# GpSimd takes the two-operand steps of the token routing, VectorE a share of the normalising, in a fused attention and mixture-of-experts kernel

## The chip, the cores and the metric
One core of a Trainium2 chip. Its engines run side by side, each with its own queue in program order: TensorE (PE, with its weight loads as PEld), VectorE (DVE), ScalarE (ACT), GpSimd (POOL), and SyncE (SP), which issues most transfers. The metric is the device time of one execution in microseconds; lower is better. TensorE's granted clock was at its upper level (1.00 of 2.4 GHz) in every 20 us of the profiled execution but the last, with a mean of 0.993.

## The reference
Causal attention for 4 batches of 12 heads, 448 tokens, head size 64. Its output, 1792 tokens of 768 values, goes through a layer of 8 experts of which each token uses one:
```python
scores = np.where(mask, -1000000000.0, scale * np.matmul(q, k.transpose(0, 1, 3, 2)))
attn = np.exp(scores - max); attn = attn / (sum(attn) + 1e-09)
x = np.matmul(attn, v)                            # per head, then 1792 x 768
logits = x @ w_gate + modality_bias[modality_id]
e_idx = np.argmax(logits, axis=1)
gate_w = softmax(logits)[np.arange(N), e_idx]
for e in range(E):
    mask = e_idx == e
    h = np.maximum(x[mask] @ w1[e], 0.0)
    out[mask] = gate_w[mask, None] * (h @ w2[e])
```

## The kernel before
The order of work is written out by hand. The attention loop has one turn n for each of the 48 heads, and each turn holds steps of several heads at once: `st_scores` of head n, `st_exp` of head n-1, `st_trans` and `st_split` of n-2, `st_pv` of n-3, `st_out` of n-4. All products are made of two parts (high and low) of each operand, so that GpSimd has to split q and k (`split_qk`, `split_kl`, one pair of heads every two turns) and v (`split_vh`, `split_vl`, every four turns). SyncE then stacks the parts of q and k by transfers within SBUF (`stack_qk`), for the scores two to four turns later, and a new q/k load starts when `split_kl` has freed one of two raw tiles.

Four heads make a group, three groups a batch. In turn n the token tile i of an older group gr (gr, i = divmod(n-8, 4)) is normalised: `st_comb` (TensorE) has put four heads' values and their share of the logits of a token tile (64 tokens in tile 0, 128 in tiles 1 to 3) in PSUM; for tiles 0 and 2 VectorE reads PSUM and multiplies by the reciprocal sums (`norm_l` for the logits, L407, `norm_x` for the values, L417); for tiles 1 and 3 ScalarE first copies them to SBUF (`st_move`, L399) and GpSimd multiplies there.

When a batch's last tile is normalised (turns 19, 31 and 43 for batches 0 to 2, after the loop for batch 3), `after_batch` spreads the steps of `route` over the turns that follow: the logits are summed, the largest found (`top`), subtracted (`centre`), the first expert among equals taken (`ties`, `first_tie`, `choice`), and TensorE counts places by matmuls with the choice (`places`). Then `slots`, `ranks` and `gates` give each token its slot in a table and its gate weight, and `scatter` writes four tables by indirect transfers on GpSimd's queue. `later(n, f)` puts a step behind the scores of turn n, `before(n, f)` ahead of them, `soon(n, f)` ahead of `st_split` of turn n; steps put at the same place run in the order in which they were put there. After batch 1 the expert with most tokens is known (`first_expert` and the following steps in turns 37 to 43), its weights are loaded, and in turns 45 to 47 GpSimd splits the first of them (`w1_chunk`, L672 and L673). Everything after about 240 us is the experts' matmuls.

Of the kernel before, what the change touches and what calls it, by code (L numbers as in the profile page):

```python
# [21 lines left out]
def attention_moe(  # L22
# [74 lines left out]
    sls = [cst(f"sl{j}", [128, NTL, E + 1]) for j in range(2)]  # L97
# [297 lines left out]
    def st_move(gr, i):  # L395
        if i % 2:
# [39 lines left out]
    def route(b):  # L436
        lg = sm([128, NTL, E], "lg")
        m = sm([128, NTL], "m")
        eq = sm([128, NTL, E], "eq")
        m2 = sm([128, NTL], "m2")  # L440
        oh = sm([128, NTL, E], "oh", BF16)
        pe = sm([128, NTL, E], "pe")
# [11 lines left out]
        def centre():  # L454
            V.tensor_tensor(out=lg, in0=lg, in1=wide(m), op=ALU.subtract)

        def ties():
            V.scalar_tensor_tensor(out=eq, in0=lg, scalar=0.0, in1=e8, op0=ALU.is_ge, op1=ALU.mult)
# [4 lines left out]
        def choice():  # L463
            V.tensor_tensor(out=oh, in0=eq, in1=wide(m2), op=ALU.is_equal)
            V.memset(oh[64:128, 0, :], 0.0)

        def places():
# [13 lines left out]
            A.activation(out=pe, in_=lg, func=AF.Exp)  # L481
            rt[b] = (pc, si)

        def slots():
            V.tensor_tensor(
# [4 lines left out]
        def ranks():  # L490
            V.tensor_reduce(out=sr, in_=sl, axis=AX, op=ALU.add)
            V.tensor_scalar(out=zs, in0=zs, scalar1=1e-9, scalar2=None, op0=ALU.add)

        def gates():
            V.tensor_copy(si, sr)
            V.reciprocal(out=ent[:, b, :, 1].bitcast(F32), in_=zs)
# [8 lines left out]
        sr = sm([128, NTL], "sr")  # L505
        return (logits, top, centre, ties, first_tie, choice), places, (slots, ranks, gates), scatter
# [29 lines left out]
    def first_base():  # L536
        V.tensor_scalar(out=eboff, in0=ebneg, scalar1=now[:, 2:3], scalar2=None, op0=ALU.add)
        V.tensor_scalar(out=eb64, in0=ebneg, scalar1=now[:, 3:4], scalar2=None, op0=ALU.add)
# [18 lines left out]
    def first_tri():  # L557
        V.tensor_scalar(out=n0, in0=oh0, scalar1=-1.0, scalar2=1.0, op0=ALU.mult, op1=ALU.add)
        V.tensor_tensor(out=tri0, in0=ctri, in1=eb(n0, E), op=ALU.mult)

    def first_order():
        V.tensor_tensor(out=tri0, in0=tri0, in1=eb(oh0, E), op=ALU.add)
        V.tensor_tensor(out=tri0, in0=tri0, in1=n0.rearrange("p (e o) -> p e o", o=1).to_broadcast([128, E, E]), op=ALU.mult)
# [310 lines left out]
    with tc.manual_schedule():  # L874
# [49 lines left out]
        V.memset(onesf, 1.0)  # L924
        V.memset(sch_a, -float(NT))
# [3 lines left out]
        for j in range(2):  # L929
            V.memset(sls[j], 0.0)  # L930
# [477 lines left out]
```

## Time and profile before
| | us |
|---|---|
| three timed executions | 504.43, 504.71, 505.88 |
| median | 504.71 |
| the profiled execution | 501.38 |
| its span, from the first to the last instruction | 499.7 |

Engines' busy time in the span: PE 476.8 us (95%), DVE 301.4 (60%), ACT 279.6 (56%), POOL 239.7 (48%). These are means over two parts: up to about 200 us, attention, in which PE, DVE, ACT and POOL are all busy for most of the time, and the experts after it, in which PE alone is. In rows of the profile a name such as L407 is a line of the kernel, `out<-in` are tiles by their names, and `[1.38 <-DVE oh L465]` says that the engine had been idle for 1.38 us until that instruction released it.

### The profile page before, as it was taken

To read this page: it belongs to the slowest core of one execution; us is meant where nothing else is said; L and a number is where in the kernel's file an instruction comes from. 1 tells how busy PE (TensorE), PEld (TensorE's weight loads), DVE (VectorE), ACT (ScalarE), POOL (GpSimd) and SP (SyncE) were. 2 spreads that over 40 slices of the span, in tenths; PEclk is the share of its full clock that TensorE was granted. 3 is DMA by queue.
4 is the path that set the end of the run, shared out by engine and by line. 5 is a ranking of instruction groups with operands and counts; after the bars stand their busy time and mean duration, and the time that the engine had idled before them with its cause. 6 is when DMAs were issued, how large, how long until landed. Compare 5 with 4: busy or idle time off the path is not lost.

```text
span 499.7 us, 10352 instructions
## 1 busy us (share of the span) xinstructions
PE 476.8 (95%) x3359; PEld 441.5 (88%) x3359; DVE 301.4 (60%) x893; ACT 279.6 (56%) x690; POOL 239.7 (48%) x292
## 2 busy tenths in 40 slices
PE   8999999999999988999999999999999999999990
PEld 5798999989988967878999999999999999888770
DVE  7899999999999999888412027441121120283580
ACT  5799999999988977616311216522121211383670
POOL 5899999999999889760311103202001001021131
PEclk9999999999999999999999999999999999999997
DMA  6887789987987889572396303863001001076100
GB/s 179 237 220 199 194 221 271 276 208 203 287 213 197 175 196 307 183 130 51 109 380 241 98 1 112 285 238 98 32 1 55 33 1 64 31 282 228 62 15 6
DMA packets 43817, 78.92 MB, mean 158 GB/s; under 512 B 15582, under 2 KB 27614, under 8 KB 43744
## 3 DMA queue, kind: packets, MB, share of 16 engines
q1 hardware_dynamic: 40704, 67.06, 47.5%
q0 software_dynamic: 3040, 11.03, 6.4%
q8 instruction: 28, 0.46, 0.4%
q14 instruction: 45, 0.37, 0.3%
HBM read 48.10 MB, written 11.89 MB: 120 GB/s over the span
## 4 chain that ended last, share of the span: by engine, by line
PE 71%; DVE 14%; DMA 6%; issue 3%; ACT 2%; POOL 1%; DVEq 0%; POOLq 0%; SPq 0%; ACTq 0%
PE g L748 7%; PE g L749 7%; PE g L750 7%; PE pt L297 6%; PE sb L266 4%; PE sa L266 4%; PE ot L336 3%; PE ot L329 3%; PE x L389 3%; DVE pl L316 3%; DVE p L275 2%; PE ot L750 2%; PE ot L749 2%; PE x L750 2%; PE x L749 2%
## 5 line engine op out<-in xcount | busy, mean ns | idle before, releaser
L285 ACT ACTIVATE p<-p,nm 128x448 f32<-128x448 f32 x192 | 94.8, 498 | 3.4 <-DVE nm L275 3.4
L729 POOL DMA_INDIRECT xg<-xs,idg x18 | 20.9, 1161 | 157.6 <-DVEq L1318 79.3
L767 DVE SCALAR_TENSOR_TENSOR htl<-g,hth 128x256 fp32r<-128x256 f32 x40 | 16.7, 424 | 103.8 <-ACT hth L766 103.8
L748 PE MATMUL g<-xh,w1h 128*128 128x256 f32 x240 | 67.1, 280 | 0.5 <-DVE htl L767 0.5
L749 PE MATMUL g<-xl,w1h 128*128 128x256 f32 x240 | 67.0, 279 | 0.0
L750 PE MATMUL g<-xh,w1l 128*128 128x256 f32 x240 | 67.0, 279 | 0.0
L297 PE MATMUL pt<-ident,p 128*128 128x128 f32 x432 | 63.2, 273 | 0.0
L316 DVE TENSOR_TENSOR pl<-pt,ph 128x1024 fp32r<-128x1024 f32 x48 | 58.3, 1215 | 7.0 <-ACT ph L315 6.8
L329 PE MATMUL ot<-ph,vhl 128*128 128x448 f32 x192 | 50.1, 301 | 3.9 <-DVE ut L360 3.7
L315 ACT ACTIVATE ph<-pt 128x1024 fp32r<-128x1024 f32 x48 | 49.0, 1020 | 7.8 <-PE pt L297 7.3
L297 PEld LDWEIGHTS pt<-ident,p 128*128 128x128 f32 x432 | 52.1, 147 | 1.2 <-issue 0.2
L766 ACT ACTIVATE hth<-g 128x256 fp32r<-128x256 f32 x40 | 15.1, 384 | 62.8 <-PE g L750 62.8
L748 PEld LDWEIGHTS g<-xh,w1h 128*128 128x128 f32 x240 | 45.1, 188 | 0.7 <-DVE htl L767 0.7
L749 PEld LDWEIGHTS g<-xl,w1h 128*128 128x128 f32 x240 | 45.1, 188 | 0.0
L750 PEld LDWEIGHTS g<-xh,w1l 128*128 128x128 f32 x240 | 45.1, 188 | 0.0
L808 POOL DMA_INDIRECT out_dram<-row,idg x14 | 16.4, 1173 | 59.6 <-ACTq L1302 33.5
L329 PEld LDWEIGHTS ot<-ph,vhl 128*128 128x128 f32 x192 | 32.8, 190 | 7.0 <-DVE ut L360 5.7
L275 DVE CUSTOM_DVE_ANT_0 p<-sa,mask 128x448 f32<-128x448 f32 x96 | 36.2, 413 | 2.3 <-PE sa L266 1.8
L285 ACT ACTIVATION_READ_ACCUMULATOR p<-p,nm 128x1 f32 x192 | 36.5, 190 | 0.0
L275 DVE CUSTOM_DVE_ANT_0 p<-sb,mask 128x192 f32<-128x192 f32 x96 | 36.3, 411 | 0.0
L336 PE MATMUL ot<-pl,vhl 128*64 128x64 f32 x192 | 34.4, 294 | 0.0
L354 ACT ACTIVATE hol<-ot 64x448 f32<-64x448 f32 x48 | 26.0, 542 | 11.2 <-PE ot L329 9.6
(348 smaller groups left out, 1340.1 us busy)
## 6 DMA issues: line engine op xcount, KB each, us to landing
st<-hl SPq DMA_DIRECT2D x56, 224.0 KB
raw<-in_moe_w_dram SPq DMA_DIRECT2D x24, 512.0 KB
raw<-in_qk_dram SPq DMA_DIRECT2D x21, 448.0 KB
raw<-in_moe_w_dram SPq DMA_DIRECT2D x20, 384.0 KB
vraw<-in_v_dram SPq DMA_DIRECT2D x12, 384.0 KB
xs<-row SPq DMA_DIRECT2D x12, 384.0 KB
w1h<-hl SPq DMA_DIRECT2D x14, 224.0 KB
w1l<-hl SPq DMA_DIRECT2D x14, 224.0 KB
```

The lines of the kernel that those rows point to most:

```text
L266: nc.tensor.matmul(outs[i], lhsT=a[:, q0:q0 + n], rhs=z[:, :w], start=(last == 0), stop=(last == 1 or qh is None))
L275: V.tensor_tensor_reduce(out=z, in0=o, in1=m, scale=-scale, scalar=3.0e38, op0=ALU.add, op1=ALU.min, accum_out=nm[:n, i:i + 1],)
L285: A.activation(out=z, in_=z, func=AF.Exp, bias=nm[:n, i:i + 1], scale=-1.0, accum_out=sums[:n, b, i, h:h + 1],)
L297: nc.tensor.transpose(out=o, in_=a, identity=ident)
L315: A.activation(out=ph, in_=t, func=AF.Copy)
L316: V.tensor_tensor(out=pl, in0=t, in1=ph.bitcast(F32), op=ALU.subtract)
L329: nc.tensor.matmul(o[:, q0:S], lhsT=t[:rows, kt, h].rearrange("p a d -> p (a d)"), rhs=ph[:rows, c0:c1], start=(n == 0), stop=(n == 1),)
L336: nc.tensor.matmul(o[0:D, q0:S], lhsT=t[:rows, kt, h, 0], rhs=pl[:rows, c0:c1], start=False, stop=False)
L354: A.activation(out=t, in_=ov[g][64:128, :S], func=AF.Copy)
L748: nc.tensor.matmul(o, lhsT=ah, rhs=bh, start=first, stop=False)
L749: nc.tensor.matmul(o, lhsT=ah, rhs=bl, start=False, stop=False)
L750: nc.tensor.matmul(o, lhsT=al, rhs=bh, start=False, stop=last)
```

## The change
In the loop's batches 0 to 2 GpSimd does the steps `ties` (with the subtraction that was `centre`), `choice` and the product of `slots`; batch 3 has the same code on VectorE. Two constants with a ninth column take the place of steps: `eq` holds 0.5 there, so that unused tokens get no choice without a memset, and `pe` holds 1e-9, so that the sum needs no addition. `ranks` reduces by the maximum straight into integers, so `gates` goes. `first_base`, `first_tri` and `first_order` move to GpSimd. Token tile 1 is normalised by VectorE from PSUM, except in the last two groups. The steps of the choice are placed at turns n+1 (two), n+2, ahead of n+3, and n+3.
```diff
     def st_move(gr, i):
-        if i % 2:
+        if i == 3 or i == 1 and gr >= B * NG - 2:
...
     def route(b):
         lg = sm([128, NTL, E], "lg")
+        G = V if b == B - 1 else P
...
-        def centre():
-            V.tensor_tensor(out=lg, in0=lg, in1=wide(m), op=ALU.subtract)
-
         def ties():
-            V.scalar_tensor_tensor(out=eq, in0=lg, scalar=0.0, in1=e8, op0=ALU.is_ge, op1=ALU.mult)
+            G.tensor_tensor(out=lg, in0=lg, in1=wide(m), op=ALU.subtract)
+            G.tensor_scalar(out=eq[:, :, 0:E], in0=lg, scalar1=0.0, scalar2=0.0, op0=ALU.is_equal, op1=ALU.add)
+            G.tensor_tensor(out=eq[:, :, 0:E], in0=eq[:, :, 0:E], in1=e8v, op=ALU.mult)
...
         def choice():
-            V.tensor_tensor(out=oh, in0=eq, in1=wide(m2), op=ALU.is_equal)
-            V.memset(oh[64:128, 0, :], 0.0)
+            ev = eq[:, :, 0:E]
+            G.tensor_tensor(out=ev, in0=ev, in1=wide(m2), op=ALU.subtract)
+            G.tensor_scalar(out=oh, in0=ev, scalar1=0.0, scalar2=0.0, op0=ALU.is_equal, op1=ALU.add)
...
         def slots():
-            V.tensor_tensor(
+            G.tensor_tensor(
                 out=sl[:, :, 0:E], in0=pc[:, 0:NP].rearrange("p (t e) -> p t e", e=E), in1=oh, op=ALU.mult
             )
             V.tensor_reduce(out=zs, in_=pe, axis=AX, op=ALU.add)
 
         def ranks():
-            V.tensor_reduce(out=sr, in_=sl, axis=AX, op=ALU.add)
-            V.tensor_scalar(out=zs, in0=zs, scalar1=1e-9, scalar2=None, op0=ALU.add)
-
-        def gates():
-            V.tensor_copy(si, sr)
+            V.tensor_reduce(out=si, in_=sl, axis=AX, op=ALU.max)
             V.reciprocal(out=ent[:, b, :, 1].bitcast(F32), in_=zs)
...
+        choose = ((1, logits), (1, top), (2, ties), (-3, first_tie), (3, choice))
+        return choose, places, (slots, ranks), scatter
...
     def first_base():
-        V.tensor_scalar(out=eboff, in0=ebneg, scalar1=now[:, 2:3], scalar2=None, op0=ALU.add)
-        V.tensor_scalar(out=eb64, in0=ebneg, scalar1=now[:, 3:4], scalar2=None, op0=ALU.add)
+        P.tensor_scalar(out=eboff, in0=ebneg, scalar1=1.0, scalar2=now[:, 2:3], op0=ALU.mult, op1=ALU.add)
+        P.tensor_scalar(out=eb64, in0=ebneg, scalar1=1.0, scalar2=now[:, 3:4], op0=ALU.mult, op1=ALU.add)
...
     def first_tri():
-        V.tensor_scalar(out=n0, in0=oh0, scalar1=-1.0, scalar2=1.0, op0=ALU.mult, op1=ALU.add)
-        V.tensor_tensor(out=tri0, in0=ctri, in1=eb(n0, E), op=ALU.mult)
+        P.tensor_scalar(out=n0, in0=oh0, scalar1=-1.0, scalar2=1.0, op0=ALU.mult, op1=ALU.add)
+        P.tensor_tensor(out=tri0, in0=ctri, in1=eb(n0, E), op=ALU.mult)
...
+        V.memset(eq, 0.5)
...
+            V.memset(pes[j], 1e-9)
...
+            (7, cast(e8v, e8)), (7, lambda: V.memset(e8v[64:128, 0], 0.0)),
...
-            for j, f in enumerate(choose, 1):
-                (later if j % 2 else before)(n + 1 + j // 2, f)
+            for j, f in choose:
+                later(n + j, f) if j > 0 else before(n - j, f)
```
`first_order` (two operations on 128x64) moves from V to P in the same way.

## Rows read from the trace of the kernel before
**Rows 1.** Chain of waits, 0 to 300 us: start, us, what
```profile
79.33 0.64 PE x L389 x4
...
95.52 0.64 PE x L389 x4
...
111.31 0.63 PE x L389 x4
...
126.48 0.64 PE x L389 x4
...
144.17 0.64 PE x L389 x4
...
197.95 0.63 PE x L389 x4
```

**Rows 2.** Windows, 91:169 us: length, busy PE, PEld, DVE, ACT, POOL, clock, DMA
```profile
91.00:169.00 78.00, 76.45 (x607) 70.12 (x607) 75.17 (x248) 70.98 (x205) 73.73 (x88) 1.00 0.85 229
```

**Rows 3.** Waits of POOL for data, 24 to 197 us: total, times, longest
```profile
POOL hl L191 <- DMA raw<-in_qk_dram: 3.3, 2, 2.7
```

**Rows 4.** Timeline of POOL, DVE and PE, 192 to 197 us: start, us, instruction
```profile
192.88 1.05 POOL L672 TENSOR_SCALAR w1h<-raw 128x1024 fp32r<-128x1024 f32 x1
194.02 2.35 POOL L673 TENSOR_TENSOR w1l<-raw,w1h 128x1024 fp32r<-128x1024 f32 x1
...
194.64 1.77 DVE L464 TENSOR_TENSOR oh<-eq,m 128x32 bf16<-128x32 f32 x1
...
196.59 0.18 PE L475 MATMUL x<-oh,upper 128*128 128x32 bf16 x1 [1.38 <-DVE oh L465]
```

**Rows 5.** Timeline of POOL, DVE and PE, 91 to 192 us
```profile
91.78 0.94 POOL L191 TENSOR_SCALAR hl<-raw 128x896 fp32r<-128x896 f32 x1 [0.61 <-DMA raw<-in_qk_dram]
...
168.56 0.93 POOL L191 TENSOR_SCALAR hl<-raw 128x896 fp32r<-128x896 f32 x1
...
176.80 0.94 POOL L191 TENSOR_SCALAR hl<-raw 128x896 fp32r<-128x896 f32 x1 [2.67 <-DMA raw<-in_qk_dram]
...
179.01 0.44 PE L266 MATMUL sa<-st 128*128 128x448 f32 x1 [1.36 <-DMA st<-hl]
...
191.28 0.61 DVE L275 CUSTOM_DVE_ANT_0 p<-sa,mask 128x448 f32<-128x448 f32 x1
...
191.47 1.07 POOL L729 DMA_INDIRECT xg<-xs,idg  x1 [0.15 <-DVE eq L458]
```

**Rows 6.** Groups of DVE by form, 0 to 290 us: busy us, mean ns, idle before
```profile
L407 DVE TENSOR_TENSOR ltp<-x,rec 128x32 f32<-128x32 f32 x11 | 1.9, 171 | 0.0
...
L417 DVE TENSOR_TENSOR row<-x,rec 128x256 f32<-128x256 f32 x11 | 4.5, 406 | 0.0
...
L464 DVE TENSOR_TENSOR oh<-eq,m 128x32 bf16<-128x32 f32 x4 | 2.9, 716 | 0.1
L455 DVE TENSOR_TENSOR lg<-lg,m 128x32 f32<-128x32 f32 x4 | 2.7, 674 | 0.0
L492 DVE TENSOR_SCALAR zs<-zs 128x4 f32<-128x4 f32 x4 | 2.4, 588 | 0.0
...
L537 DVE TENSOR_SCALAR eboff<-ebneg,now 128x8 f32<-128x8 f32 x1 | 1.2, 1231 | 0.0
L563 DVE TENSOR_TENSOR tri<-tri,n 128x64 f32<-128x64 f32 x1 | 1.2, 1192 | 0.0
...
L963 DVE CAST evals<-row 128x32 f32<-128x32 int32 x1 | 0.5, 470 | 0.0
```

**Rows 7.** Groups of POOL by form, whole span
```profile
L417 POOL TENSOR_TENSOR row<-cxt,rec 128x256 f32<-128x256 f32 x22 | 13.5, 612 | 0.0
...
L407 POOL TENSOR_TENSOR ltp<-cxt,rec 128x32 f32<-128x32 f32 x22 | 5.2, 239 | 2.1 <-ACT cxt L399 2.1
...
L993 POOL TENSOR_SCALAR row<-row 128x16 f32<-128x16 f32 x2 | 0.6, 300 | 0.2
...
L1216 POOL TENSOR_TENSOR mask<-ident 128x64 f32<-128x64 f32 x1 | 0.3, 340 | 0.0
```

More of the change, by code (lines that the diff above doesn't have):

```diff
@@ L96, in attention_moe @@
     lts = [ltp[:, j] for j in range(2)]
-    sls = [cst(f"sl{j}", [128, NTL, E + 1]) for j in range(2)]
+    sls, pes = ([cst(f"{x}{j}", [128, NTL, E + 1]) for j in range(2)] for x in ("sl", "pe"))
+    eq = cst("eq", [128, NTL, E + 1])
+    e8v = cst("e8v", [128, NTL, E])
     ent = cst("ent", [128, B, NTL, 2], I32)
@@ L437, in route @@
         lg = sm([128, NTL, E], "lg")
+        G = V if b == B - 1 else P
         m = sm([128, NTL], "m")
-        eq = sm([128, NTL, E], "eq")
         m2 = sm([128, NTL], "m2")
         oh = sm([128, NTL, E], "oh", BF16)
-        pe = sm([128, NTL, E], "pe")
+        pe = pes[b % 2]
         pc = sm([128, NP + E], "pc")
@@ L480, in places @@
             A.activation(out=pc, in_=pos[:, 0:NP + E], func=AF.Copy)
-            A.activation(out=pe, in_=lg, func=AF.Exp)
+            A.activation(out=pe[:, :, 0:E], in_=lg, func=AF.Exp)
             rt[b] = (pc, si)
         def slots():
-            V.tensor_tensor(
+            G.tensor_tensor(
                 out=sl[:, :, 0:E], in0=pc[:, 0:NP].rearrange("p (t e) -> p t e", e=E), in1=oh, op=ALU.mult
@@ L503, in scatter @@
                 )
-        sr = sm([128, NTL], "sr")
-        return (logits, top, centre, ties, first_tie, choice), places, (slots, ranks, gates), scatter
+        choose = ((1, logits), (1, top), (2, ties), (-3, first_tie), (3, choice))
+        return choose, places, (slots, ranks), scatter
     def eb(a, x):
@@ L557, in first_tri @@
     def first_tri():
-        V.tensor_scalar(out=n0, in0=oh0, scalar1=-1.0, scalar2=1.0, op0=ALU.mult, op1=ALU.add)
-        V.tensor_tensor(out=tri0, in0=ctri, in1=eb(n0, E), op=ALU.mult)
+        P.tensor_scalar(out=n0, in0=oh0, scalar1=-1.0, scalar2=1.0, op0=ALU.mult, op1=ALU.add)
+        P.tensor_tensor(out=tri0, in0=ctri, in1=eb(n0, E), op=ALU.mult)
     def first_order():
-        V.tensor_tensor(out=tri0, in0=tri0, in1=eb(oh0, E), op=ALU.add)
-        V.tensor_tensor(out=tri0, in0=tri0, in1=n0.rearrange("p (e o) -> p e o", o=1).to_broadcast([128, E, E]), op=ALU.mult)
+        P.tensor_tensor(out=tri0, in0=tri0, in1=eb(oh0, E), op=ALU.add)
+        P.tensor_tensor(out=tri0, in0=tri0, in1=n0.rearrange("p (e o) -> p e o", o=1).to_broadcast([128, E, E]), op=ALU.mult)
     def schedule_a(cnt):
@@ L1233, in attention_moe @@
         choose, places, rank, scatter = after_batch(B - 1, 0)
-        for f in choose:
+        for _, f in choose:
             f()
```

## The prediction
> **What bounds the kernel now.** I read the chain of waits first. A block of four heads (turns of the attention loop) ends each time with the combining matmuls of the first token tile, L389 on 64 rows, so the distance from one such row to the next but three is the price of four heads. From 111.31 to 126.48 it is 15.17 us, and the chain is TensorE alone there [rows 1]. Three blocks are longer: 79.33 to 95.52 is 16.19 (1.02 over), 95.52 to 111.31 is 15.79 (0.62 over), 126.48 to 144.17 is 17.69 (2.52 over). These are the blocks in which batches 0 and 1 are routed. From 144.17 to 197.95 lie three blocks, 53.78 us, 8.27 over 3 x 15.17. So at most 12.4 us can be won in this part, and some of that is the routing's own matmuls, which stay.
>
> Second, the windows: in attention all four compute engines are nearly full. VectorE is busy 75.17 of the 78 us from 91 to 169, GpSimd 73.73 [rows 2]. Third, the waits of GpSimd: between 24 and 197 us it waits for data only 3.3 us, twice, both times for a q/k load [rows 3]. That is the view I rest on. GpSimd isn't the bound in the blocks at 15.17, but it never rests, so wherever VectorE is sped up, GpSimd's queue is what comes next.
>
> Fourth, the timeline where attention ends. VectorE's L464 (the choice of batch 2) runs 1.77 us, from 194.64 to 196.41, and GpSimd's L673, a weight split, ends at 196.37; TensorE has then waited 1.38 us for the choice [rows 4]. A VectorE operation with two SBUF operands thus stands until GpSimd's running instruction is through. The Trainium skill ("SBUF — State Buffer", section "SBUF: two separate sides") says that such operations and GpSimd's share one port pair as an exclusive lock, held for a whole instruction; the trace agrees, with those 1.77 us.
>
> **VectorE.** The change takes away the operations that show this stall: L455, L464 and L492 (four times each, means 674, 716 and 588 ns for some 32 elements or fewer), L537 and L563 (1231 and 1192 ns, once) [rows 6]. An undisturbed one lasts as long as L407, 171 ns on 128x32 [rows 6]. So in the three batches inside the loop these lines alone give back about 6 us of waiting, with the smaller ones that go along (ties, the integer copy, `first_tri`) some 8. It adds L407 and L417 for token tile 1 in ten blocks, 171 + 406 ns, 5.8 us [rows 6], spread evenly. It also adds a cast of `e8` in turn 7: 0.17 us if free, 0.47 as the like cast of `evals` beside GpSimd [rows 6], and four small memsets; that part of the loop is full on VectorE, so I take +0.3 us, early, where the slower steady blocks later let GpSimd catch up. ScalarE loses ten copies, and nothing waits for them after the change.
>
> **GpSimd.** Removed: ten pairs L407 + L417, 0.239 + 0.612 = 0.85 us each, 8.5 us [rows 7]. Added per batch: two-operand operations on 128x32, which I price as L407, 0.239, and comparisons with a constant, priced as L993, 0.300, with 0.1 before an operation that needs the one ahead (L993 shows 0.2 for two) [rows 7]. `ties` is 0.239 + 0.3 + 0.239 + 2 x 0.1 = 0.98, `choice` 0.239 + 0.3 + 0.1 = 0.64, `slots` 0.24: 1.86 per batch, 5.6 for three. Once: `first_base` 2 x 0.3, `first_tri` 0.3 + 0.34 + 0.1, `first_order` 2 x 0.34 + 0.1 with L1216's 0.340 for 128x64 [rows 7]: 2.1. Sum 7.7 against 8.5. **On the queue that is next in line the change nearly pays for itself and no more.** Bounds: 0.171 for each two-operand operation (VectorE's) below, 0.340 (L1216, twice the elements) above; I take 0.239, the same shape on the same engine. The Trainium skill ("GPSIMD Engine Reference", section "Engine selection") warns against this very move: elementwise work with two inputs is about twice as slow there. By that a 128x32 operation would be 2 x 0.171 = 0.34 us, as my upper end; the rows show 0.239 against 0.171 for the same operation, 1.4 times, and the row decides.
>
> Now the path. GpSimd's first wait, 0.61 us, ends at 91.78 (turn 22) and its second, 2.67 us, at 176.80 (turn 42) [rows 5]. The load that ends it could start only when the split before 168.56 had freed its buffer; the same backlog makes TensorE wait 1.36 us for the stacked q/k at 179.01 [rows 5]. From 176.80 GpSimd runs without a gap, through the weight splits, to 196.37, and then TensorE gets the choice. So between 91.78 and 196.6 the end of attention is set by GpSimd's queue plus one load. What changes on it:
> - pairs of turns 25, 29, 33, 37, 45 gone: 5 x 0.85 = -4.25 (those of 21 and 41 lie in front of the two waits and only lengthen them);
> - `slots` of batches 0 and 1: +0.48; `ties` of batches 1 and 2: +1.96; `choice` of both: +1.28; `first_order`: +0.78. `first_base` and `first_tri` fall before the 2.67 us wait, which covers their 1.34 us; without that wait they cost that;
> - `ties` and `choice` of batch 0: 1.62 into 0.61 + 0.85 of wait: +0.16;
> - the hand-over: TensorE starts 0.22 us after the split now, about 0.06 after the choice then: -0.16.
>
> Sum +0.25. Against it stand the pairs of turns 9, 13 and 17, up to 2.55 us of lead, as far as the load that ends at 91.78 comes earlier with them. I take half, 1.3: **-1.0 us**. Bounds: +0.25 with none kept, -2.3 with all.
>
> VectorE's own gain reaches TensorE in turns 23 to 40, but TensorE then stands longer before the q/k of turn 44; the late next thing is that load.
>
> **The new waits.** `first_tie` on VectorE now waits for `ties` on GpSimd, and behind it queue the row maxima of the next head, for which ScalarE's exponentials and the scores bank wait. In batches 0 and 1 it has over half a turn of slack. In batch 2 `ties` is issued behind a weight split and the gather at 191.47 [rows 5], so it ends near 193, where VectorE began those maxima at 191.28 [rows 5]: it waits about 2 us, but no longer stands 1.77 us later [rows 4].
>
> **The last batch** stays on VectorE, after attention: one operation more ahead of its matmuls and two fewer behind, each near 0.2 us. Its first wait moves 0.2 later, its second 0.4 earlier: nothing. Everything behind is matmuls without gaps.
>
> **The rivals.**
> - VectorE decides after all (0.30): GpSimd's lead is kept and the two loads come sooner, since the 8 us for the second one are long. Then the 4.2 us over in the three routing blocks mostly go [rows 1] and part of the last 8.27: about -4 us, 500.7. For it: the stalls are plain. Against it: rows 3.
> - Batch 2's routing behind the weight splits (0.20), the one on the other side. With no lead kept, `ties` ends at 191.47 + 1.07 + 0.98 = 193.5 [rows 5], VectorE resumes 2.3 us later than now, the scores of head 47 follow, and the choice comes at 193.5 + 0.3 + 0.64 and a split of 3.49 (192.88 to 196.37 [rows 4]) = 197.9 instead of 196.5. With two-operand operations at their upper end and the early +0.3 it is +2 us, 506.7. It decides when GpSimd's lead at 176.80 is below about 1.3 us.
> - The forecast, GpSimd's queue sets the end (0.50).
>
> **How the numbers follow.** The profiled execution took 501.38 us (span 499.7), the three timed ones 504.43 to 505.88. The sum, -1.0, is made on the profiled one and carried to the median 504.71: 503.7. No change, as far as a measurement of this kernel can tell, is 0.3%, 1.5 us. Of the forecast's 0.50, 0.40 is within that, 0.07 faster, 0.03 slower; the first rival's 0.30 is faster; of the second's 0.20, 0.15 is slower and 0.05 within. So faster 0.37, same 0.45, slower 0.18. The range goes from the first rival's 500.7, a little beyond, to just short of the second's: 500.2 to 506.2; the forecast's own is 502.4 to 505.
>
> **What would show it.** Right: L275's neighbours on VectorE without operations of 0.5 to 1.8 us; blocks of 15.2 to 16 us up to turn 40 and then a longer wait of TensorE for the stacked q/k of turn 44; GpSimd still without pauses but for two loads; `first_tie` of batch 2 preceded by a wait of VectorE for GpSimd; the choice of batch 2 within 1.5 us of where it is now. Wrong: if the wait at 176.80 has shrunk and the choice comes before 194, the first rival holds; if GpSimd's new operations last 0.4 us or more, or the wait in batch 2 exceeds 2.5 us, the second.

## The result, and the profile after

The changed kernel takes 507.61 us (median of 16 executions, 504.85 to 510.48), the kernel before on the same chip 503.64 (16 executions, 502.24 to 506.63). The ratio is 1.0066, 95% interval 1.0047 to 1.0086: slower by some 3.3 us, beyond the upper end of the predicted range. The profiled execution took 505.53 us, span 503.8; all the numbers of the profile below are from it.

The loss isn't spread out. TensorE starts the scores of turn 36 at 143.85 (before: 144.73) and those of turn 43 at 172.23 (172.86), so up to there the changed kernel is ahead. Turn 44 starts at 180.72 (179.01), turn 45 at 186.94 (182.82). At turn 45 the changed kernel is 4.12 us behind; turn 46 gives some of that back (190.66 for 187.78, 2.88 behind), and about 3 us stay to the end of attention and behind it: the place on the chain of waits that stood at 229.50 (the first L750 there, now L748) stands at 232.86.

The timeline of POOL, DVE and PE in the changed kernel, 91 to 200 us, answers to [rows 4, 5] (lines have moved by two or so: L193 was L191, L268 was L266, L670 and L671 were L672 and L673, L477 was L475):

```profile
93.05 0.95 POOL L193 TENSOR_SCALAR hl<-raw 128x896 fp32r<-128x896 f32 x1 [1.17 <-DMA w1l<-hl]
...
168.90 0.93 POOL L193 TENSOR_SCALAR hl<-raw 128x896 fp32r<-128x896 f32 x1
...
178.53 0.94 POOL L193 TENSOR_SCALAR hl<-raw 128x896 fp32r<-128x896 f32 x1 [3.60 <-DMA raw<-in_qk_dram]
...
180.72 0.71 PE L268 MATMUL sa<-st 128*128 128x448 f32 x1 [4.38 <-DMA st<-hl]
...
183.62 0.42 DVE L419 TENSOR_TENSOR row<-x,rec 64x256 f32<-64x256 f32 x1 [5.80 <-DMA xs<-row]
...
194.18 0.25 POOL L457 TENSOR_TENSOR lg<-lg,m 128x32 f32<-128x32 f32 x1
...
195.22 0.19 DVE L462 TENSOR_REDUCE m<-eq 128x4 f32<-128x36 f32 x1 [2.12 <-POOL eq L459]
...
196.68 2.38 POOL L671 TENSOR_TENSOR w1l<-raw,w1h 128x1024 fp32r<-128x1024 f32 x1
...
199.34 0.32 POOL L467 TENSOR_SCALAR oh<-eq 128x32 bf16<-128x32 f32 x1
...
199.72 0.18 PE L477 MATMUL x<-oh,upper 128*128 128x32 bf16 x1 [0.46 <-POOL oh L467]
```

Four of these rows stand against four of before and cut the way to the choice of batch 2 into stages. The predicted column is the working's own terms, sorted into the same stages.

| stage | before | after | change | predicted |
|---|---|---|---|---|
| to the split that ends GpSimd's first wait | 91.78 | 93.05 | +1.27 | -1.14 (half the lead, 1.3; batch 0, +0.16) |
| from there to the split of heads 44 and 45 | 76.78 | 75.85 | -0.93 | -1.30 (four pairs -3.40; batch 1's steps and two `slots` +2.10) |
| from there to the split of heads 46 and 47 | 8.24 | 9.63 | +1.39 | 0 ("one load") |
| from there to the choice on TensorE | 19.79 | 21.19 | +1.40 | +1.39 (pair -0.85, batch 2 +1.62, `first_order` +0.78, hand-over -0.16) |
| sum | | | +3.13 | -1.05 |

Second, the windows of the same kernel around turn 44 (length, busy PE, PEld, DVE, ACT, POOL, granted clock, DMA share, GB/s):

```profile
176.00:178.00 2.00, 0.33 (x3) 0.06 (x1) 1.83 (x3) 2.00 (x8) 0.00 (x0) 1.00 1.07 223
178.00:180.00 2.00, 0.00 (x0) 0.00 (x0) 0.00 (x0) 0.48 (x2) 1.38 (x2) 0.82 1.09 230
180.00:182.00 2.00, 1.28 (x6) 1.23 (x6) 0.00 (x0) 0.00 (x0) 1.92 (x3) 0.50 0.87 161
182.00:184.00 2.00, 2.00 (x11) 1.96 (x10) 0.38 (x2) 0.00 (x0) 2.00 (x1) 0.50 0.08 8
184.00:186.00 2.00, 2.00 (x11) 1.96 (x11) 2.00 (x12) 0.69 (x1) 1.92 (x6) 0.50 0.66 223
186.00:188.00 2.00, 2.00 (x17) 1.92 (x17) 1.94 (x4) 1.59 (x5) 2.00 (x4) 0.97 0.96 192
```

From 178 to 180 us TensorE and VectorE do nothing, while the transfers never rest. TensorE waits 4.38 us for the stacked q/k of head 44, its granted clock falls from 1.00 to 0.50, the lower of its two levels (1.2 GHz), and stays there until about 186. Turn 44 therefore lasts 6.22 us (180.72 to 186.94), before 3.81. In the kernel before the wait is 1.36 us [rows 5] and the clock stays at 1.00. The mean clock of all 16 timed executions of the changed kernel lies between 0.978 and 0.986, that of the kernel before, in its executions beside the runs below, between 0.984 and 0.994; so the fall belongs to the kernel and not to this one execution.

Third, why that q/k is late. SyncE's queue in the kernel before, 160 to 178 us (start, us, instruction; L209 stacks head 42 and 43's parts, L664 loads expert weights, L208 stacks those of head 44 and 45, L429 stores finished rows):

```profile
160.81 0.62 SPq L209 DMA_DIRECT2D w1l<-hl  x1
163.12 0.36 SPq L664 DMA_DIRECT2D raw<-in_moe_w_dram  x1
...
164.74 0.41 SPq L664 DMA_DIRECT2D raw<-in_moe_w_dram  x1
...
169.52 0.47 SPq L208 DMA_DIRECT2D st<-hl  x1
...
177.97 0.47 SPq L429 DMA_DIRECT2D xs<-row  x1
```

and in the changed kernel:

```profile
161.16 2.17 SPq L211 DMA_DIRECT2D w1l<-hl  x1
164.53 0.36 SPq L662 DMA_DIRECT2D raw<-in_moe_w_dram  x1
...
166.16 0.41 SPq L662 DMA_DIRECT2D raw<-in_moe_w_dram  x1
...
169.86 0.47 SPq L210 DMA_DIRECT2D st<-hl  x1
...
179.65 0.47 SPq L431 DMA_DIRECT2D xs<-row  x1
```

One issue takes 2.17 us in place of 0.62, and the two weight loads behind it (0.5 MB each) leave 1.4 us later. The second now leaves 3.70 us ahead of the stacking of heads 44 and 45 and not 4.78, and that stacking, which starts 0.34 later, lands 1.7 later. The store of batch 2's first rows leaves 1.68 later as well, and VectorE, which wants that row buffer in turn 44, stands until 183.62 (before: 181.67).

What the prediction said of single operations held up to 206 us. GpSimd's groups by form, 20 to 206 us (busy us, mean ns, idle before), against the prices 239, 300 and 340 ns from [rows 7]:

```profile
L458 POOL TENSOR_SCALAR eq<-lg 128x32 f32<-128x32 f32 x3 | 1.0, 346 | 0.3
L467 POOL TENSOR_SCALAR oh<-eq 128x32 bf16<-128x32 f32 x3 | 1.0, 322 | 0.3
L459 POOL TENSOR_TENSOR eq<-eq,e8v 128x32 f32<-128x32 f32 x3 | 0.7, 248 | 0.3
L457 POOL TENSOR_TENSOR lg<-lg,m 128x32 f32<-128x32 f32 x3 | 0.7, 242 | 0.0
L466 POOL TENSOR_TENSOR eq<-eq,m 128x32 f32<-128x32 f32 x3 | 0.7, 239 | 1.0 <-DVE m L462 0.9
L487 POOL TENSOR_TENSOR sl<-pc,oh 128x32 f32<-128x32 f32 x2 | 0.5, 241 | 0.0
```

The product of batch 2's `slots` comes later, at 211.72 us, and takes 1.23 us. In the rows above the two-operand operation on 128x32 takes 239 to 248 ns on GpSimd and 193 in batch 3 on VectorE, 1.25 to 1.3 times. The Trainium skill ("GPSIMD Engine Reference", section "Engine selection") has about twice; the direction agrees with this trace, the size doesn't.

### The profile page after: what moved, and what is told of

It reads as the page before. It is cut to its first block, busy times and chain, and to the rows that moved or that the text cites. A ratio compares the mean times of both kernels' runs of the same rounds, so it can differ in the third digit from the quotient of the medians.

```text
span 503.8 us, 10342 instructions
## 1 busy us (share of the span) xinstructions
PE 478.8 (95%) x3359; PEld 444.6 (88%) x3359; DVE 295.2 (59%) x890; ACT 276.7 (55%) x680; POOL 239.0 (47%) x296
## 4 chain that ended last, share of the span: by engine, by line
PE 65%; POOL 10%; DVE 9%; DMA 7%; issue 5%; ACT 1%; POOLq 0%; DVEq 0%; SPq 0%; ACTq 0%
PE g L748 7%; PE g L746 7%; PE g L747 7%; PE pt L299 5%; PE sb L268 3%; PE sa L268 3%; DMA st<-hl 3%; PE ot L338 3%; PE ot L331 2%; PE x L391 2%; PE ot L748 2%; PE ot L747 2%; PE x L748 2%; PE x L747 2%; PE x L746 2%
## 5 line engine op out<-in xcount | busy, mean ns | idle before, releaser
L748 PE MATMUL g<-xh,w1l 128*128 128x256 f32 x240 | 67.2, 280 | 0.0
L748 PEld LDWEIGHTS g<-xh,w1l 128*128 128x128 f32 x240 | 45.1, 188 | 0.0
```

The source lines that it names most:

```text
L748: nc.tensor.matmul(o, lhsT=al, rhs=bh, start=False, stop=last)
```

## The experiments

All are ratios to the kernel before, run beside it on the same chip, with 95% intervals of about a quarter of a per cent either way, in some runs up to 0.45; so two runs are told apart from about a third of a per cent on. A profile shows one execution, and executions of one kernel differ by several us (502.24 to 506.63 for the kernel before), so a time read from a trace can stand well beside the median of its run.

| run | ratio | interval |
|---|---|---|
| the change | 1.0066 | 1.0047 to 1.0086 |
| e1_batch2_vector | 1.0043 | 1.0019 to 1.0067 |
| e2_warm_head44 | 1.0034 | 1.0008 to 1.0059 |
| e3_no_gpsimd_routing | 0.9981 | 0.9957 to 1.0005 |
| e4_tile1_back | 1.0164 | 1.0118 to 1.0209 |
| e5_after_later_weights | 1.0051 | 1.0024 to 1.0078 |
| e6_before_later_weights | 1.0104 | 1.0064 to 1.0145 |
| e7_batch2_vector_warm | 1.0038 | 1.0007 to 1.0068 |
| e8_no_routing_later_weights | 0.9977 | 0.9953 to 1.0001 |
| e9_after_two_more_rows | 1.0058 | 1.0025 to 1.0091 |
| e10_after_rows_later_weights | 1.0047 | 1.0023 to 1.0072 |
| e11_before_two_more_rows | 0.9985 | 0.9963 to 1.0007 |
| e12_before_rows_later_weights | 1.0077 | 1.0045 to 1.0108 |
| e13_batch1_vector | 1.0001 | 0.9973 to 1.0028 |
| e14_batches12_vector | 1.0002 | 0.9981 to 1.0023 |
| e15_no_routing_rows | 0.9985 | 0.9966 to 1.0004 |
| e16_slots_only | 1.0076 | 1.0050 to 1.0103 |
| e17_before_tile1 | 0.9932 | 0.9908 to 0.9956 |
| e18_before_tile1_rows | 0.9942 | 0.9918 to 0.9967 |

### Which queue sets the end

**e3_no_gpsimd_routing.** On the changed kernel, all routing back on VectorE in its rewritten form:

```diff
-        G = V if b == B - 1 else P
+        G = V
```

and `first_base`, `first_tri`, `first_order` on `V` again.

> The changed kernel with all its routing operations and first_base, first_tri and first_order on VectorE; token tile 1 is still normalised by VectorE, slots still come out as integers. GpSimd has 7.7 us less, VectorE stands behind GpSimd again. Theory 'GpSimd's queue sets the end': faster than the changed kernel by 3 to 5 us (502.6 to 504.6). Theory 'VectorE's load decides': slower than the changed kernel by 1 to 4 us.

Measured: 0.9981, 0.85% (4.3 us) less than the change. VectorE is busy 3.9 of every 4 us from 172 to 192, TensorE doesn't wait for the stacked q/k, and the clock stays at 1.00. Putting the routing back on VectorE made the kernel faster, so rival one, VectorE decides, falls as it was put. That VectorE's work costs nothing does not follow: e16 and e17 below show that it does.

**e4_tile1_back.** On the changed kernel, token tile 1 back on ScalarE and GpSimd:

```diff
-        if i == 3 or i == 1 and gr >= B * NG - 2:
+        if i % 2:
```

> The changed kernel with token tile 1 copied by ScalarE and normalised by GpSimd in all groups again; the routing stays on GpSimd. GpSimd has 8.5 us more, VectorE 5.8 us less. Theory 'GpSimd's queue sets the end': slower than the changed kernel by 3 to 5 us. Theory 'VectorE's load decides' (the added normalising is what costs): faster than the changed kernel by 1 to 3 us.

Measured: 1.0164, 0.98% (4.9 us) more than the change. GpSimd's split of heads 44 and 45 starts at 173.43 in place of 168.90. Work taken from GpSimd wins and work given to it loses, as the forecast's view of its queue has it. That its queue alone sets the end is not shown: e3 and e17 below have the same 272 instructions on GpSimd and differ by 0.49%.

### Batch 2 and the clock

**e1_batch2_vector.** On the changed kernel, batch 2's routing on VectorE:

```diff
-        G = V if b == B - 1 else P
+        G = V if b >= B - 2 else P
```

> The changed kernel with batch 2 routed on VectorE as batch 3 is; batches 0 and 1 stay on GpSimd. Theory 'batch 2 behind the weight splits': VectorE no longer waits 2.1 us for ties ahead of head 46 and GpSimd's queue is 1.6 us shorter, so turn 46 lasts 4.3 to 4.6 us instead of 5.5, and the time falls by 1.5 to 2.5 us against the changed kernel (507.6 to about 505.6). Theory 'the halved clock in turn 44': that turn still lasts 6.2 us and the time falls by less than 1 us.

Measured: 1.0043. The wait of `first_tie` (2.12 us) is gone, but TensorE's wait for the stacked q/k is 5.3 us, its clock 0.55 to 0.60 from 180 to 188, and the choice comes at 201.82, later than in the changed kernel. The execution traced took 507.32 us, the longest of the run's twelve (median 505.74). By the ratios about a third of the loss is gone, 0.23%; the intervals tell that neither from nothing nor from most of the loss. So this run alone doesn't decide on the rival, which named batch 2's place behind the weight splits.

**e2_warm_head44.** On the changed kernel, products that keep TensorE busy while it would wait:

```diff
+        for _ in range(80 if g == 44 else 0):
+            nc.tensor.matmul(banks[0][:, 0:128], lhsT=ones, rhs=ones, start=True, stop=True)
```

> The changed kernel with 80 small extra matmuls (their result is overwritten) ahead of the scores of head 44, in the 4.4 us in which TensorE waits for the stacked q and k. Theory 'the halved clock in turn 44': the granted clock stays at 1.00, turn 44 lasts 3.8 instead of 6.2 us, and the time falls by 2 to 2.4 us. Theory 'GpSimd's queue sets the end of attention': the clock stays up too, but the choice of batch 2 still comes out of GpSimd's queue at about the same moment, TensorE waits longer for it, and the time is the changed kernel's within 0.5 us.

Measured: 1.0034, 0.32% (1.6 us) less than the change. Two windows of its profile (columns as above) show TensorE busy and at the upper level where it idled and then ran at 0.50:

```profile
180.00:182.00 2.00, 2.00 (x35) 1.99 (x33) 0.00 (x0) 0.00 (x0) 1.92 (x3) 1.00 0.72 142
182.00:184.00 2.00, 2.00 (x20) 1.98 (x19) 0.68 (x2) 0.00 (x0) 2.00 (x2) 1.00 0.16 20
```

Turn 44 lasts 3.70 us again, although it starts as late (181.63). The choice of batch 2 still comes at 199.45 (199.72 in the changed kernel), as the queue theory said, but the time moved by more than the 0.5 us that it allowed. So the halved clock is probably a part of the loss, about 0.3%; with the two intervals overlapping, that share is not shown beyond doubt.

**e7_batch2_vector_warm.** Both edits together.

> The changed kernel with batch 2's routing on VectorE and 80 products of ones ahead of head 44's scores (the two edits of the runs e1_batch2_vector and e2_warm_head44 together; the products are of no use to the result). If the choice behind the weight splits (1.9 us alone) and the halved clock of turn 44 (2.6 us alone) are two separate losses, they add: 503.1, the time of the kernel before. If they are the same microseconds seen twice (with a faster turn 44 TensorE only waits longer for the choice): 504.5 to 505, no better than the warm clock alone.

Measured: 1.0038, no better than the warm clock alone. The two don't add. What is left with both is the late start of turn 44, 181.07 against 179.01 before.

### Where the lateness of turn 44 comes from

**e5_after_later_weights** (on the changed kernel) and **e6_before_later_weights** (on the kernel before) issue the first two weight loads three turns later:

```diff
-        W1AT = (8, 9, 14, 14, 15, 15)
+        W1AT = (11, 12, 14, 14, 15, 15)
```

> The changed kernel with its first two loads of expert weights (0.5 MB each) issued in turns 42 and 43 in place of 39 and 40, so that they stand on SyncE's queue behind the q/k load of heads 46 and 47 and the stacking transfers of head 44, not ahead of them. Theory A (the loss of turns 44 to 47 comes from transfers: the stacked q/k of head 44 landed 1.7 us later than before because the weight loads, issued 1.4 us later than before, took their time from it): TensorE's wait for it, 4.38 us, falls below 2 us, its clock stays at 1.00, turn 45 starts near 184 and not at 186.94, and the time falls by 3 to 5 us against the changed kernel, to 503 to 504.5. Theory B (the loss is GpSimd's queue alone, with the choice of batch 2 behind the weight splits): the wait may shrink, but the choice still comes within 1 us of 199.7 and the time stays within 1 us of 507.6.

> The same shift of the two weight loads in the kernel before, whose wait for the stacked q/k of head 44 is 1.36 us and whose GpSimd waits 2.67 us for the load of heads 46 and 47. Theory A: both waits go, 1 to 2.5 us won, 501 to 502.5. Theory B (GpSimd's queue from there to the choice): what GpSimd no longer waits, up to 2.67 us, is won as well if nothing else is late, so a gain here speaks for both; no gain (within 0.5 us) speaks against A and says that the transfers' lateness is covered in this kernel.

Measured: 1.0051 and 1.0104, so one is no better than the change within the intervals and the other loses 1%, which neither theory had. The profile of the first shows both halves of the answer (timeline of PE and DVE, 177 to 194 us):

```profile
177.31 0.44 PE L268 MATMUL sa<-st 128*128 128x448 f32 x1 [1.48 <-DVE ut L362]
...
181.14 0.47 PE L268 MATMUL sa<-st 128*128 128x448 f32 x1
...
193.52 0.42 DVE L419 TENSOR_TENSOR row<-x,rec 128x256 f32<-128x256 f32 x1 [4.91 <-DMA xs<-row]
```

Turn 44 starts at 177.31 and turn 45 at 181.14, 3.4 and 5.8 us sooner than in the changed kernel, the clock at 1.00: it was the weight loads that kept the stacked q/k. But the loads now lie ahead of the stores of finished rows, and VectorE stands 4.91 us for one of those. The transfers of this stretch are one queue, and moving the large ones only chooses who waits.

**e8_no_routing_later_weights** is the same shift on e3_no_gpsimd_routing.

> No routing step on GpSimd (as in the run e3_no_gpsimd_routing: token tile 1 on VectorE and the integer slots stay) with the two weight loads in turns 42 and 43. Where no operation of the routing lies on GpSimd, GpSimd is ahead (its split of heads 44 and 45 starts at 166.7 and not 168.9) and TensorE does not wait for the stacked q/k. If transfers matter only where they are waited for: no change against that run, 503 within 1 us. If the wait of GpSimd for the load of heads 46 and 47 (2.82 us there) still sets the choice: 1 to 2.5 us less, 500.5 to 502.

Measured: 0.9977, against 0.9981 without the shift: where turn 44 waits for nothing, moving the loads changes nothing that can be measured.

**e9 to e12** take the stores' wait away with two more row buffers, in unused weight tiles:

```diff
-            xrow[b, i] = row()
+            xrow[b, i] = raw1[K1 - 1 - i][:, 0:DM] if b == B - 2 and i < 2 else row()
```

e9_after_two_more_rows is the changed kernel with them, e10_after_rows_later_weights has the shifted loads too, e11 and e12 are the same two edits on the kernel before.

> The changed kernel with two more row buffers for the normalised values (tiles 0 and 1 of batch 2 lie in raw1[5] and raw1[4], which are free then), so that VectorE's normalising of tile 0 in turn 44 does not wait for the store of batch 2's tile 0; that wait was 5.80 us and ended at 183.62 (before: 0.77, 181.67). Theory C (turn 44 is late because SyncE's queue is late: the store stands behind eight index reads, and VectorE stands behind the store): VectorE's wait goes, head 44's maxima start 2 to 3 us sooner, 1.5 to 3 us won against the changed kernel, 504.5 to 506. Theory A (TensorE's own wait for the stacked q/k and its halved clock set turn 44, VectorE's wait lies beside them): less than 1 us won, 506.5 to 507.6.

> The changed kernel with the two more row buffers and with the first two weight loads in turns 42 and 43 (as in the run e5_after_later_weights, where the wait for the stacked q/k went and VectorE then stood 4.91 us for the store of tile 1). If transfers (stacking and stores together) are the whole loss: neither wait is left, the clock stays at 1.00, turn 47 starts near 191.5 to 193, the choice of batch 2 comes by 196.5, and the time is 502.5 to 504, as before or a little under. If GpSimd's queue with the choice behind the weight splits is a loss of its own: first_tie of batch 2 waits 2 us or more and the time stays at 505 or above.

> The kernel before with the two more row buffers. Its VectorE waits only 0.77 us for the store, and what follows, the choice at 196.4, waits for GpSimd's port: within 0.8 us of 503.3 by either theory. More than 1.5 us won would say that the store was a bound in the kernel before as well.

> The kernel before with both edits, the control for e10_after_rows_later_weights. If the loss from the weight loads alone in the kernel before (6.7 us, run e6_before_later_weights) came from the stores behind them, most of it goes: 502 to 505. The difference to e10_after_rows_later_weights is then what the change itself is worth where no transfer is waited for: by the prediction's queue sum 0 to 2 us less for the changed kernel, by the loss in batch 2 alone 1 to 2 us more.

Measured: 1.0058, 1.0047, 0.9985 and 1.0077. In e9 VectorE no longer waits for the store in turn 44; it waits 3.56 us for TensorE's scores instead, which start at half clock after 3.94 us of waiting for the stacked q/k. The store thus lay beside the q/k wait and was not the cause. e10 and e12 are misses: the buffers cover tiles 0 and 1, and the third tile's store, now behind a weight load, holds VectorE for 6.23 and 4.29 us in turn 46. They don't give the control that they were meant to give.

**e13_batch1_vector.** On the changed kernel only batch 1's routing goes back to VectorE:

```diff
-        G = V if b == B - 1 else P
+        G = V if b in (1, B - 1) else P
```

> The changed kernel with only batch 1's routing steps (turns 33 to 36) back on VectorE; batches 0 and 2 stay on GpSimd. Theory D: batch 1's steps put GpSimd's q/k splits of turns 32 to 36 about 1 us late, the loads and stacking transfers that follow come closer together, SyncE's last stacking issue of head 42 then stands 2.17 us (0.62 before), the weight loads are issued 1.4 us later and lie in the way of head 44's stacking. Then here that issue lasts 0.62 again, the weight loads go out 4.5 us or more ahead of head 44's stacking (3.70 in the changed kernel, 4.78 before), TensorE's wait is below 2.5 us, the clock stays at 1.00 and the time is 503.5 to 505.5. If the lateness comes from batch 2 or from TensorE's running ahead alone: the issue lasts 2 us, the wait 4 us or more, and the time is within 1 us of the changed kernel, 506.5 to 508.

Measured: 1.0001; with one of three batches back on VectorE no loss is left that the times show. SyncE's queue in it (same lines as above) has the short stacking issue and the early first weight load of the kernel before:

```profile
160.98 0.62 SPq L211 DMA_DIRECT2D w1l<-hl  x1
163.15 0.36 SPq L662 DMA_DIRECT2D raw<-in_moe_w_dram  x1
...
165.78 0.42 SPq L662 DMA_DIRECT2D raw<-in_moe_w_dram  x1
169.68 0.47 SPq L210 DMA_DIRECT2D st<-hl  x1
```

and TensorE starts turn 44 without a wait to be seen:

```profile
178.91 0.44 PE L268 MATMUL sa<-st 128*128 128x448 f32 x1
```

Its clock is 1.00 from 176 to 188. The short issue, the wait and the time are as theory D asked, but the second weight load leaves 3.90 us ahead of the stacking of heads 44 and 45 (165.78 to 169.68), not 4.5 or more, and the clock falls later on. Its mechanism isn't there either: GpSimd's splits and SyncE's issues of the two kernels lie within 0.2 us of each other from 150 to 161 us (the q/k load at 154.63 here, at 154.80 in the changed kernel, 0.1 us behind a stacking issue in both), so nothing is closer together. Nor is GpSimd's queue much shorter: with 1.86 us of batch 1's steps gone, its split of heads 44 and 45 starts 0.18 us sooner (168.72 for 168.90), since from 90 to 169 us it now waits 1.8 us for q/k loads and in the changed kernel for none. What differs is TensorE, which starts turns 36 to 43 some 2.5 us later here, and the moment at which a block of instructions is loaded. The queue q8, which moves instructions, has one transfer of 0.02 MB in this stretch (queue, packets, MB, share of the 16 engines); in the changed kernel it is in 161 to 162 us, at the long issue:

```profile
q8 instruction: 1, 0.02, 12.1%
```

and here in 164 to 165, where another issue, that of a v load, stands in its place:

```profile
164.07 1.51 SPq L235 DMA_DIRECT2D vraw<-in_v_dram  x1
```

The instructions that come here are TensorE's and not SyncE's. The changed kernel has 28 such transfers in all, and e2, which adds nothing but products on TensorE, has 29 (lines of the two pages):

```profile
q8 instruction: 28, 0.46, 0.4%
```

```profile
q8 instruction: 29, 0.48, 0.4%
```

From 368 to 422 us of the changed kernel three of them pass while SyncE has no instruction at all. And the tenth, the one here, starts in every one of the twenty traces when TensorE has begun 2478 to 2509 of its matmuls and weight loads. So a TensorE that is 2.5 us ahead fetches it sooner, at 161.06 in the changed kernel and at 164.10 here, and 161.06 is the moment of SyncE's stacking issue.

From 157 to 172 us every issue of 1.2 us or more has the transfer beside it. It comes within about a microsecond of the start of a long stacking issue (1.89 to 2.31 us) in the changed kernel and in e1, e2, e4, e5, e7, e9 and e10, and of a long issue of a v or weight load (1.24 to 1.51 us) in e13, e15, e17 and e18. In the kernel before and in e3, e6, e8, e11, e12, e14 and e16 no issue within a microsecond of it takes more than 0.7 us, though in e14 and e16 some start while it runs. From 24 to 200 us of all twenty traces, the 15 issues of 1.8 us or more all start within 0.8 us of a transfer of q8; of the 105 of 1.2 us or more only 64 lie within a microsecond of one, so shorter stands have other causes too. A block of the other instruction queue, q14, comes within 0.2 us of the long stacking issue as well in six of the eight kernels; in e4 and e9 it doesn't, so the transfer of q8 is what all eight share. In e13 the first weight load has already left when the code comes, and the transfers keep moving (windows 162 to 164 and 170 to 172 of the changed kernel, then of this one; the last two columns are the DMA share and GB/s):

```profile
162.00:164.00 2.00, 2.00 (x20) 1.97 (x19) 2.00 (x10) 1.53 (x7) 2.00 (x3) 1.00 0.52 153
170.00:172.00 2.00, 2.00 (x20) 1.97 (x19) 1.94 (x11) 1.85 (x5) 2.00 (x4) 1.00 1.22 119
```

```profile
162.00:164.00 2.00, 2.00 (x15) 1.57 (x15) 2.00 (x10) 1.85 (x3) 1.89 (x3) 1.00 0.94 241
170.00:172.00 2.00, 2.00 (x19) 1.96 (x18) 2.00 (x9) 1.98 (x4) 2.00 (x4) 1.00 0.37 36
```

The transfers lose half of the two microseconds from 162 on, and the backlog is still there when the stacking of heads 44 and 45 leaves. Turn 36 starts at 146.30, 2.45 us later than in the changed kernel, and turn 44 at 178.91, 1.81 us sooner: TensorE's lead in turns 33 to 43, which batch 1's move buys, is worth nothing, since the q/k of turn 44 comes when the transfers let it.

The execution of e13 that was traced took 506.36 us, the longest of its twelve (median 504.04), and it shows what the move of batch 1 leaves in place. VectorE's `first_tie` of batch 2 waits 2.07 us for GpSimd's ties, TensorE then waits 2.12 us for VectorE until turn 47 starts at 194.35, and the clock falls a second time:

```profile
196.00:198.00 2.00, 2.00 (x12) 1.67 (x11) 1.94 (x9) 0.28 (x2) 1.91 (x4) 0.55 0.77 309
198.00:200.00 2.00, 2.00 (x14) 1.83 (x15) 0.45 (x4) 1.24 (x3) 1.89 (x4) 0.50 0.90 280
```

The choice comes at 198.38 (before 196.59, changed kernel 199.72). So in this execution the rival's mechanism, batch 2 behind the weight splits, does cost time.

**e14_batches12_vector.** Only batch 0 stays on GpSimd (`G = P if b == 0 else V`).

> Batches 1 and 2 on VectorE, only batch 0 on GpSimd (and first_base, first_tri, first_order, which stay there). If the losses of batch 1 (transfers) and of batch 2 (choice behind the weight splits, 1.9 us in the run e1_batch2_vector) are two: 1 to 2 us less than e13_batch1_vector, 502.5 to 504. If batch 2 costs only what turn 44's lateness makes of it: within 0.8 us of e13_batch1_vector.

Measured: 1.0002, as e13: with batch 1 on VectorE, the times show no cost of batch 2's place behind the weight splits, within intervals that leave room for a microsecond or two. In the one execution traced the wait for the ties is gone and the choice comes at 195.94, 2.44 us sooner than in that of e13.

### What the other parts are worth

**e16_slots_only** is e3_no_gpsimd_routing with tile 1 back on GpSimd, so only the rewritten steps are left. **e17_before_tile1** is the kernel before with tile 1 alone:

```diff
     def st_move(gr, i):
-        if i % 2:
+        if i == 3 or i == 1 and gr >= B * NG - 2:
```

**e18_before_tile1_rows** adds the two row buffers to that, **e15_no_routing_rows** adds them to e3_no_gpsimd_routing.

> As e3_no_gpsimd_routing, but token tile 1 is back on ScalarE and GpSimd: what is left of the change is the integer slots, the ninth columns and the turns of the steps. If relieving GpSimd of tile 1 is what makes e3_no_gpsimd_routing as fast as the kernel before or faster (GpSimd's queue sets the end): 1 to 3 us slower than that, 504 to 506. If VectorE's load sets it: VectorE loses 0.58 us in each of ten blocks, so faster, 501 to 502.5.

> The kernel before with one part of the change alone: token tile 1 normalised by VectorE, except in the last two groups; the routing as it was. With the rewritten steps, tile 1 was worth 0.95% (e16_slots_only 1.0076 to e3_no_gpsimd_routing 0.9981) and 0.98% (e4_tile1_back 1.0164 to the changed kernel, 1.0066). If that holds with the old steps too (GpSimd's queue sets the end, and GpSimd loses 8.5 us of work): 0.990 to 0.992, 498.5 to 499.5. If VectorE, with 5.8 us more work and all of its stalled operations, becomes the bound: 502.5 to 505, no faster than before. Below 500 would say that the rewritten steps, not only the move to GpSimd, are what costs the changed kernel its gain.

> The same with two more row buffers, since tile 1's wait for the store of the last batch falls to VectorE here and not to GpSimd. If that wait is not there in e17_before_tile1: the same within 0.8 us. If it is: up to 2 us less than that.

> No routing on GpSimd (run e3_no_gpsimd_routing, 503.1) with two more row buffers (which gave the kernel before 0.15%, not separable from nothing). A candidate for a version that beats both. If the store is waited for nowhere in e3_no_gpsimd_routing, which its profile says, the same 503.1 within 1 us; if the two gains add, 501.5 to 502.3.

Measured: 1.0076, 0.9932, 0.9942 and 0.9985. The row buffers add nothing. Tile 1 alone beats both kernels: 498.42 us beside 502.96 for the kernel before.

Tile 1 is worth 0.94% with routing on VectorE (0.9981 to 1.0076), 0.96% with it on GpSimd (1.0066 to 1.0164), 0.68% with the old steps. Moving the routing to GpSimd costs 0.85% with tile 1 on VectorE and 0.87% without. These two add. The rewriting itself costs 0.76% on VectorE without tile 1 and 0.49% with it (0.9932 to 0.9981). VectorE's groups of e16_slots_only, 0 to 290 us, do not show where that goes:

```profile
L459 DVE TENSOR_TENSOR eq<-eq,e8v 128x32 f32<-128x32 f32 x4 | 4.0, 996 | 0.1
L466 DVE TENSOR_TENSOR eq<-eq,m 128x32 f32<-128x32 f32 x4 | 3.5, 875 | 0.0
L457 DVE TENSOR_TENSOR lg<-lg,m 128x32 f32<-128x32 f32 x4 | 2.0, 508 | 0.0
...
L467 DVE TENSOR_SCALAR oh<-eq 128x32 bf16<-128x32 f32 x4 | 1.1, 277 | 0.1
```

There are as many operations with two SBUF operands as before, three per batch. The first stands shorter than its forerunner (508 ns for 674), the other two longer (996 for 518, 875 for 716), and two comparisons with a constant are added to each batch. Together these steps take 11.5 us in four batches. But what they replace took 11.8: 7.7 for the three like them, 2.4 for the addition that goes, 1.5 for the integer copy and 0.2 for the memset. So VectorE's busy time doesn't explain the 0.76%; the steps also stand at other turns, which no run tried by itself.

The two pairs with the same instructions on GpSimd (272 in e3 and e17, 292 in e16 and the kernel before) thus differ by 0.49% and 0.76%. What VectorE does moves the time as well, and GpSimd's queue alone doesn't set it.

## Why the prediction was wrong

**What held.** Work put on GpSimd's queue or taken from it does move the end (e3, e4); the prices of its new operations held to 50 ns up to 206 us; the last stage was forecast at +1.39 and came at +1.40, the stage with four pairs gone at -1.30 and came at -0.93; `first_tie` waits 2.12 us where about 2 was said; the ties end at 195.2 and the choice comes at 199.7, later than the 193.5 and 197.9 of the slower rival by about the 1.73 us by which the split of heads 46 and 47 is late. VectorE's relief did not show as time.

**The step that failed** is "the end of attention is set by GpSimd's queue plus one load", with a load of fixed length and a lead of which "I take half, 1.3". Both errors are one: the transfers were taken as a constant that sits behind GpSimd's queue, while here they were late for reasons of their own. The range followed the same step: it stopped at 506.2, just short of the 506.7 of the rival that keeps no lead, which had a chance of 0.20.
- The lead. In e17_before_tile1, which has the pairs of turns 9, 13 and 17 gone and nothing added on GpSimd, the load was issued 1.26 us sooner (84.47 for 85.73), and its split started at the same time:

```profile
91.66 0.95 POOL L191 TENSOR_SCALAR hl<-raw 128x896 fp32r<-128x896 f32 x1 [2.45 <-DMA raw<-in_qk_dram]
...
172.63 0.94 POOL L191 TENSOR_SCALAR hl<-raw 128x896 fp32r<-128x896 f32 x1 [2.40 <-DMA raw<-in_qk_dram]
```

  GpSimd only waits longer, 2.45 us against 0.61 [rows 5]. None of the lead is kept, at the far bound (+0.25 for the sum) and not the middle. In the changed kernel that split is even 1.27 later: `choice` of batch 0 waits 0.94 us for VectorE at 91.23, and the split then waits 1.17 us until the stacking has read the buffer that it writes. The term was -1.14 and measured +1.27.
- The load. "Plus one load" was 8.24 us from split to split and became 9.63, +1.39 against 0. The split can't start before its data have come through a queue that holds two weight loads and four stackings, and that queue was late by the one long issue. In e13, without it, the stage is 7.98 us (168.72 to 176.70), and the times show no loss. The issue stands when a block of TensorE's instructions is loaded. That every such long issue from 157 to 172 us has the load beside it is shown; that the load makes the issue stand is argued from it. The Trainium skill ("Runtime: NRT & Kernel Launch", section "Instruction fetch mechanics") says that an engine's instructions are streamed in blocks of 16 KiB by the engine's own DMA queue, and that crossing a block is mostly hidden. The traces agree with the size (0.02 MB) and with a queue that follows one engine, TensorE, by the counts of e2. Of an issue on another engine that stands beside the load, as SyncE's did in twelve of the twenty kernels traced, this says nothing.

**What the prediction didn't price** is TensorE's clock: "TensorE then stands longer before the q/k of turn 44" was written down as free. A wait of 4.38 us brought the clock to 0.50 for some 6 us and made turn 44 2.4 us longer; what that is worth in the end is about 0.3% by e2, at the edge of what its intervals tell.

**The rivals.** That VectorE's relief decides is refuted by e3; that VectorE's work counts beside GpSimd's is shown by e16 and e17. The slower rival had the right side, a condition that was met (no lead at 176.80, the split starting at 178.53) and a time, 506.7, near the measured one. Its mechanism is in the traces: the last stage is 1.40 us longer, as it and the forecast both had it, and in e13's traced execution it costs a fall of the clock too. But it isn't the whole: the split of heads 46 and 47 was already 1.73 us late, and by the times e1 gains 0.23% and e14 over e13 nothing that is told from noise. That the rival's time came near the measured one is in part luck, since the lateness and the clock were not in it.

**Smaller terms.** The early setup was +0.3 and was about +1.0 by turn 12 (50.54 for 49.54); the cast of `e8` is one of several operations that stretch there, and which of them costs wasn't tried. The last batch was "nothing" and has 0.55 us more from batch 2's choice to its own; two comparisons of 0.46 and 0.56 us on VectorE beside GpSimd's scatters, where 0.2 was said, would account for that. By experiment the parts are: tile 1 -0.68% (-3.4 us; forecast -5.55 with half the lead), the routing from its old form on VectorE to its new one on GpSimd +1.35% (1.0066 over 0.9932, +6.8 us; forecast +4.5 and +0.3 early).

**What stays open.** Whether the code load makes the issue stand, and how: the kernels with batch 1 on GpSimd and those with the load at the stacking issue are the same ones, so the cost of batch 1, 0.65%, may be partly bad luck, the cost of that place, and no run had the one without the other. Which of the rewritten steps makes e16_slots_only 0.76% slower than the kernel before was not tried one by one. Nor was the old form of the routing on GpSimd.

## What to carry to other kernels

A change of several parts is worth its parts, and here one of them alone, the tile that takes work off GpSimd, gives 0.68%, while the others take twice that back. Where a queue's end is a sum of work plus a transfer, the transfer is not a constant: ask when it is issued, what lies ahead of it on its own queue, and whether work that comes sooner only waits longer. Where one issue in a trace is much longer than its twins, look at what the instruction queues move at that moment. An engine that is let run ahead arrives early at the next thing that is late, and on TensorE that wait can cost its clock as well; it also fetches its code sooner, and what happened to lie free of that in one kernel may not in the next.

## What the runs showed of the hardware that was not expected

- The price of a TensorE wait can be more than the wait. After 4.38 us without a matmul the granted clock was 0.50 from 180 to 186 us and turn 44 lasted 6.22 us in place of 3.81. After the 1.36 us of the kernel before it stayed at 1.00; in e10 it fell to 0.50 after a wait of 1.77 us and in e13 after one of 2.12 us, while in e2 one of 2.18 us at the same place as in e13 left it at 1.00. Products of no use in the gap of turn 44 (e2) kept it at 1.00 there.
- The issue of a transfer can itself stand: the same instruction on SyncE took 0.62 us or 2.17, the long time with a transfer of TensorE's instructions beside it, and everything behind it on that queue, with no dependence on it, moved.
- Issuing a load 1.26 us sooner let the split that waits for it start 0.12 us sooner (e17).
